# An attention and gated-MLP block on one core: outputs transposed in place, head sets in pairs, and queue orders from a table

## The chip, the cores and the metric

The kernel runs on one core of a Trainium2 chip. The core has a tensor engine (PE, with its weight loads PEld), a vector engine (DVE), a scalar engine (ACT), GpSimd (POOL) and a sync engine (SP), each with an instruction queue of its own that is worked off in order. The metric is device time in microseconds, the median of several runs. The profile shows one execution; its span runs from the first to the last instruction.

## The reference, cut to what matters

One layer over 2048 tokens of width 640, with 32 heads of width 20 and a hidden width of 1536:

```
mod = silu(c) @ w_mod;  sa, ca, ga, sb, cb, gb = its six parts
h = layernorm(x) * (1 + ca) + sa
q, k, v = split(h @ wqkv)                   # 32 heads x 20
p = softmax(q @ k.T * 20 ** -0.5)           # per head, 2048 x 2048
x = x + ga * (concat(p @ v) @ wo)
h = layernorm(x) * (1 + cb) + sb
x = x + gb * (((h @ w_gate) * (h @ w_up)) @ w_down)
```

Of the work, 32 x 2048 x 2048 exponentials are the largest single part.

## The kernel before, in words

**Chunks, items, units.** Queries are cut into seven chunks (CHUNKS): one of 512 and six of 256. Heads go in eight sets of four; the four heads of a set lie in the four 32-row strips of a tile. A chunk and a set make an item (`items`), worked in order. Within an item a unit is one head's scores of 512 columns: one tile of 128 keys by 512 queries in chunk 0, two tiles of keys by 256 queries in the others. The last item is split into two halves of 128 queries (SPLITJ, with QHALF).

**Two ways to an exponential.** Scores are products of KT and QT (line 1524) into PSUM banks. Most units go to ACT: two units, 1024 columns, per instruction (line 1561, called E), written to the ring PPs. Two pairs of banks take turns, so that a score group waits for the exponential before last. QUADS says how many quads of four units in each item go to DVE instead: an eviction with a rounding into integers (line 1585, called P1) for each unit, two bit operations over the quad (1617 and 1625) and a product (1622 on DVE or, in four pieces, 1637 on POOL). A quad's result comes as two terms, and each is multiplied with V.

**Products with V.** Line 2192 multiplies the exponentials with Vf, four strips side by side, and sums them in one bank for each item (a slot of G, four banks, which also serve the quads' scores and all projections). Vf holds a column of ones in front of each head, so the sums of the softmax come with the outputs.

**The end of an item** (`item_end_tasks`). DVE transposes the bank in blocks of 32 by 32 into OT (line 1717, T1), takes reciprocals (1723), POOL or DVE multiplies (1725, into OTn), and DVE transposes back into OcT (1734). Its rows, 32 a head, have to be packed to 20 a head: `oc_pieces` cuts the item into runs of rows and one DMA on SP for each run copies it into Ocp (line 1746). A chunk has 32 heads of which four cross a border of 128 rows, so 36 copies; for the last chunk's last set there is no copy, and four products with wo7, a second, padded copy of the last rows of wo, use OcT directly. wo is loaded by one DMA (line 1492) and wo7 by four.

**The suffix of a chunk** (`suffix`): the product with wo (line 970 or 966), the second layernorm, transposes (1889), then for each of twelve columns of 128 the gate and up products, with weights brought by DMA into three staging buffers (stg, line 1931). For chunks of 256, gate and up of one column share a bank; DVE evicts the gate half to gsb (1959) and multiplies it with the up half into hprod (1966). For chunk 0 each has its own bank (1986, 1997). Then the down product and the output. It runs beside the next chunk's attention; the last chunk's runs alone, the tail of the program.

**K and Q** are projected during chunk 0 (line 1230), packed, evicted to KPA or KPB, written to DRAM (line 1276) and loaded back spread over the strips (KT by line 1289, QT by 1298), because rows of 20 have to be spread to 32. All these DMAs are issued by SP, in its order.

**Who sets the order.** A planner in the kernel, `Sched`, simulates all engines when the program is built, with a duration for each task and guesses for DMA landings; `pick_pe` chooses what PE does next, and numbers by item (STAGE) tune the choices. The outcome is a fixed order of instructions on each queue, which `emit_program` writes out with the semaphore waits between them. Where little work would be on PE for a while, `do_fill` and `zero_fill` put in products with zeros (line 2523), called fillers.

Of the kernel before, what the change touches and what calls it, by code (L numbers as in the profile page):

```python
# [13 lines left out]
SEM = 60.0  # L14
# [4 lines left out]
X_FIRST = 0.0  # L19
ACT_LAT = 250.0  # L20
# [16 lines left out]
LKTOL = 300.0  # L37


class Task:  # L40
    __slots__ = ("head", "hval", "hknow", "eng", "dur", "lat", "deps", "emits", "ctr", "prio", "gate", "acq", "on_start", "slots",
                 "start", "done", "needed", "val", "know", "nleft", "ready", "users", "name", "mode", "seq", "rt", "sem",
                 "nbytes", "cond", "alt", "land", "firm", "lk", "dead", "key")

    def __init__(self, eng, dur, emits, deps=(), ctr=None, prio=0.0, lat=None, gate=0, acq=(), on_start=None,
# [28 lines left out]
        self.dead = False  # L74
        if lat is None:
            lat = {"pe": PE_DRAIN, "act": ACT_LAT, "dve": DVE_LAT, "pool": 60.0}.get(eng, 0.0)
        self.lat = lat

# [5 lines left out]
class Slots:  # L84

    def __init__(self, ids, name=""):
        self.name = name
        self.free = [(i, []) for i in ids]
        self.hold = {}
        self.gone = set()  # L90
        self.out = {}

    def avail(self, only=None):
        best = None
        for k, (i, rel) in enumerate(self.free):
            if only is not None and i != only:
                continue
            t = 0.0
            for r in rel:
                t = max(t, r.done + SEM)  # L100
            if best is None or t < best[0]:
                best = (t, k)
        return best
# [13 lines left out]
    def done(self, i, task):  # L117
        h = self.hold[i]
# [9 lines left out]
    def add(self, i, rel):  # L128
        self.free.append((i, rel))


class Sched:

    def __init__(self):
# [28 lines left out]
        self.lk_last = None  # L163

# [39 lines left out]
    def _enable(self, task):  # L204
        t = 0.0
        for d in task.deps:
            t = max(t, d.done + SEM)
# [70 lines left out]
    def step_engine(self, eng):  # L278
        if self.free_at[eng] > self.t:
            return False  # L280
        self.pull(eng)
        rl = self.readyl[eng]
        for k, task in enumerate(rl):
# [5 lines left out]
            if self.locked(eng, task):  # L289
                continue  # L290
            if self.acquire(task, self.t):
# [63 lines left out]

def emit_program(nc, sched, nsem_dma=56):
# [23 lines left out]
    for t in sched.all:  # L380
# [11 lines left out]
        for d in deps:  # L392
            if not (d.nbytes or d.eng != eng or d.eng in ("dve", "pool")):
                continue
            if d.head and eng == "act":
# [88 lines left out]
TB_GATE = 2  # L484
# [3 lines left out]
D_LEAD = 0.451  # L488
NB0, NSS = 3, 3
XB0, XSS = 0, 0  # L490
HEADG = 1000
OP_EARLY = 1
EV_OP = 0.5
# [3 lines left out]
LN2T = 0.6  # L497
# [5 lines left out]
HOLD = 110  # L503
PVTOL = 249
XDPRIO = 1.343
# [5 lines left out]
STX_G, STX_T, STX_S, W_ISSUE = 3, 20, 1.5, 600.0  # L511
ZFILL = 1
WD_POOL, WD_PRIO = 1, 400.0
# [4 lines left out]
WM_GATE = 8  # L518
# [3 lines left out]
K_LEAD = 0.683  # L522
# [3 lines left out]
D_LATE = 16  # L526
D_RES = 20
PVMIN, PVMAX, PVCAP = 2, 7, 12
PV0 = 0
V_PARTS = [[0, 2], [2, 4], [4, 6], [6, 8]]  # L530
V_L1 = 0.2
# [10 lines left out]
GATE_F = (0.446, 0.5, 0.5, 0.5, 0.5, 0.5, 1.0)  # L542
FILL_MIN = 4190.746
# [9 lines left out]
LN2P = 0.85  # L553
NALT = 1
OPFIRST = 1500
STG_B = 0.95
ENDP, END3, P_POW = 0.4, 1, -1.0
HT_L = 0.25
V_L = 0.221
LATE_A = 2.065  # L560
LATE_L = 1.418
LATEQ = (2, 3)
LATEQ_A = -20
LATEQ_F = 0.35
# [4 lines left out]
    0: {"PVMIN": 2, "HOLD": 95, "PVTOL": 249, "D_RES": 58, "PVCAP": 6, "X_HALF": 0.0, "XDPRIO": 1.343, "FILL_MIN": 3463.3, "LKTOL": 300.0, "EAGER": 9, "PVMAX": 14, "X_LATE": -179.96, "TPRIO": 0.75, "STEAL_GAP": 200, "D_LATE": 16, "PV_KEEP": 2},  # L569
    1: {"PVCAP": 15, "XBACK": 1, "FILL_MIN": 4629.7},  # L570
    2: {"DL": 0.376},
    4: {"HOLD": 58.0, "X_LATE": -39.3},
    5: {"D_LATE": 7, "PVMAX": 3},
    6: {"X_LATE": 168.4, "FILL_MIN": 5225.9, "HOLD": 156.4},
    7: {"DL": 0.501},
    8: {"FILL_MIN": 2868.8},
    10: {"X_HALF": 69.3, "HOLD": 73.7, "PVMAX": 5},
    11: {"DL": 0.443},
    12: {"DL": 0.459, "HOLD": 108.3, "X_LATE": 6.6},
    13: {"DL": 0.417},  # L580
    15: {"X_LATE": 86.8},
    16: {"HOLD": 135.0, "FILL_MIN": 4362.5},
    17: {"X_LATE": -17.4, "LKTOL": 338.9, "HOLD": 52.0},
    19: {"DL": 0.471, "PVMAX": 7, "HOLD": 113.6},
    20: {"DL": 0.391, "PVMAX": 10},
    21: {"X_LATE": -85.4, "PVMIN": 3},
    24: {"DL": 0.464, "STEAL_GAP": 210.6, "X_LATE": -52.5, "PVCAP": 14, "HOLD": 116.4, "LKTOL": 98.1},
    25: {"DL": 0.549, "LKTOL": 370.4, "HOLD": 156.3},
    26: {"DL": 0.411, "PVMIN": 1, "X_LATE": 2.0, "EAGER": 6, "X_HALF": 58.0},
    27: {"DL": 0.473},  # L590
    29: {"HOLD": 148.6, "D_LATE": 5, "LKTOL": 267.5, "D_RES": 36, "PVMAX": 3},
    30: {"EAGER": 11},
    31: {"X_LATE": -99.6, "HOLD": 173.2, "X_HALF": 164.9, "PV_KEEP": 2},
    33: {"DL": 0.442, "PVMIN": 7, "PV_KEEP": 3, "X_HALF": 147.4},
    34: {"PVMIN": 3, "X_HALF": 26.9, "STEAL_GAP": 91.8, "EAGER": 8, "X_LATE": 136.8, "D_RES": 25},
    35: {"X_HALF": 148.7},
    36: {"DL": 0.524},
    37: {"FILL_MIN": 4112.0, "EAGER": 8, "X_LATE": -201.5},
    39: {"STEAL_GAP": 162.9, "EAGER": 9},
    42: {"PVMAX": 8, "FILL_MIN": 4334.4, "PV_KEEP": 3},  # L600
    43: {"HOLD": 127.6},
    46: {"D_LATE": 20, "PV_KEEP": 3, "X_LATE": -80.9},
    53: {"LKTOL": 820.1, "X_HALF": 73.5},
    54: {"PVTOL": 279.6, "FILL_MIN": 4011.5, "X_HALF": 31.3},
}
XHALF = 1
STG_G0, STG_G, XC_G = 12, -10, -20
X_LATE = -24.052
X_HALF = 0.0
# [10 lines left out]
def build_kernel(nc, A_x, A_wqkv, A_wo, B_x, B_w_gate, B_w_up, B_w_down, c, w_mod, out):  # L620
# [96 lines left out]

    PPs = [alloc("PP", [128, NPS, w * 512], BF16) for w in ((3, 2) if HEADG < 1000 else (2, 2))]
    wo7 = alloc("wo7", [128, D], BF16)
# [9 lines left out]
    OTn = alloc("OTn", [128, 512], BF16)  # L729
    NOC = 2  # L730
    OcT = alloc("OcT", [128, NOC, 512], BF16)
    oc_off = region(2 * KD * 512 * 2)
    Ocp = at("Ocp", [128, 2, KD, 512], BF16, oc_off)
# [6 lines left out]
    late_off = region(late_size)  # L740
    early_off = region(early_size)
    R1 = Sub(late_off, late_size)
# [4 lines left out]
    R1 = Sub(early_off, early_size)  # L747
# [5 lines left out]
    R2 = Sub(early_off, early_size)  # L753
    hprod = R2.alloc("hprod", [128, FT, 512], BF16)
    h2T = R2.alloc("h2T", [128, KD, 512], BF16)
    xck = R2.alloc("xck", [128, 4, D], BF16)
    xn2 = R2.alloc("xn2", [128, 4, D], BF16)
# [8 lines left out]
    KPB = alloc("KPB", [128, 2, 512], BF16)  # L766
# [30 lines left out]
    G = Slots([5, 6, 2, 7], "G")  # L797
    GX = Slots([3, 4] if HEADG else [2, 3, 4], "GX")
    hx = (1, 3) if HEADG else (1, 3, 4)
    GC = Slots([0, 1], "GC")  # L800
    setA = Slots([0], "A")
    setB = Slots([0], "B")
    pPs = [Slots(list(range(NPS)), "PP") for _ in range(2)]

    def ring():
        return len(pPs[0].free) + len(pPs[1].free)
# [3 lines left out]
    sOcT = Slots(list(range(NOC)), "OcT")  # L810
# [407 lines left out]
    def k_base(tc):  # L1218
        return 80 if tc in K_DIRECT else 0
# [87 lines left out]
    def v_round(t, pt, prio, gate=0):  # L1307
        a, z = V_PARTS[pt]
        nh = 4 * (z - a)
        w = nh * DH  # L1310
        mms = []
        for k in range(KD):
            f = quarters(w, lambda k=k: hT[t // 4][:, k, t % 4 * 128:t % 4 * 128 + 128],
                         lambda k=k: wV[:, k, 80 * a:80 * a + w], k == 0, k == KD - 1)
            mms.append((X(w), f))

        def after(r):
            dst = Vf[:, (t * H + 4 * a) * VW:(t * H + 4 * a + nh) * VW].rearrange("p (h w) -> p h w", w=VW)[:, :, 1:VW]
            f = lambda e: e.tensor_copy(dst, ps[:, r.b["b"], 0:w].rearrange("p (h w) -> p h w", w=DH))
# [1309 lines left out]
```

## Time and profile before

| what | value |
|---|---|
| median of 3 runs | 806.06 us (804.76 to 808.96) |
| span of the profiled execution | 803.8 us |
| exponentials on ACT (line 1561) | 810, first start 16.4 us, last start 774.7 us |
| quads' evictions on DVE (line 1585) | 428, in 285.5 us |
| quads' products on POOL (line 1637) | 268 pieces, in 305.0 us |
| copies of line 1746 of the commonest size | 164, of 10.0 KB each |
| bytes moved by DMA | 64.66 MB, mean 80 GB/s |

Times are microseconds from the span's start. PE is the matrix products, PEld its weight loads; "SPq" is the queue of SP, on which it issues DMAs. An instruction's group is named by its line, what it writes and what it reads. A busy PE is not a PE at its peak, since products overlap.

### The profile page before, as it was taken

The page shows a single profiled execution, that of the slowest core. Times are in us where ns is not written, and L with a number is a line of the kernel's source. Part 1 is how long each engine was busy: PE and PEld are TensorE (multiplying, and loading weights), DVE is VectorE, ACT ScalarE, POOL GpSimd, SP SyncE. Part 2 cuts the span into 40 slices and gives each one's busy share as a digit, 9 for nine tenths or more (in the row PEclk, how much of TensorE's full clock was granted, in tenths as well). Part 3 has the DMA queues.
Part 4 walks back from the last instruction along what each step waited for, and adds up shares of the span by engine and source line. Part 5 has one row for each costly group of instructions (what it writes and reads, how often), then busy time and mean ns, then how long its engine had stood idle before and what let it go on. Part 6 is the DMA issues. An engine that isn't in the chain of part 4 may idle for free.

```text
span 803.8 us, 37761 instructions
## 1 busy us (share of the span) xinstructions
PE 790.4 (98%) x16595; PEld 380.6 (47%) x16595; DVE 697.8 (87%) x1401; ACT 764.8 (95%) x847; POOL 386.0 (48%) x396
## 2 busy tenths in 40 slices
PE   8999999999999999999999999999999999999998
PEld 4433433333244434445555455555555555555567
DVE  7978788799989999988999999999899988898754
ACT  6899899999999999999999999999999999999961
POOL 3347455654366565763444443545534554455300
PEclk9999999999999999999999999999999999999999
DMA  9733212212341532120032404231540254414420
GB/s 297 243 113 91 62 43 64 61 33 76 92 109 50 167 88 52 35 55 13 24 81 65 95 16 112 57 73 39 121 89 15 54 118 94 98 37 106 92 68 18
DMA packets 154314, 64.66 MB, mean 80 GB/s; under 512 B 116951, under 2 KB 154151, under 8 KB 154151
## 3 DMA queue, kind: packets, MB, share of 16 engines
q1 hardware_dynamic: 153223, 61.10, 30.0%
q8 instruction: 132, 2.16, 1.1%
q10 hardware_dynamic: 928, 1.15, 0.5%
q14 instruction: 31, 0.25, 0.1%
HBM read 50.63 MB, written 8.99 MB: 74 GB/s over the span
## 4 chain that ended last, share of the span: by engine, by line
PE 77%; ACT 14%; DVE 5%; issue 2%; DMA 1%; SPq 1%; POOL 0%; DVEq 0%; ACTq 0%
PE ps_all L1524 26%; PE ps_all L970 21%; PE ps_all L2192 19%; ACT PP L1561 14%; PE ps_all L1230 4%; PE ps_all L966 3%; DVE DB L1585 2%; PE ps_all L1889 1%; PE ps_all L1166 1%; PE ps_all L1127 1%; DVE DSS L1617 1%; PE ps_all L2523 0%; DVE DSS L1625 0%; DMA QT<-q_rows 0%; PE ps_all L991 0%
## 5 line engine op out<-in xcount | busy, mean ns | idle before, releaser
L1561 ACT ACTIVATE PP<-ps_all 128x1024 bf16<-128x1024 f32 x810 | 748.5, 1090 | 6.7 <-PE ps_all L1524 4.8
L1637 POOL TENSOR_TENSOR DSS<-DB,DSS 128x512 bf16<-128x512 bf16 x268 | 305.0, 1157 | 290.6 <-DVE DSS L1625 254.2
L1585 DVE TENSOR_SCALAR DB<-ps_all 128x512 int16<-128x512 f32 x428 | 285.5, 681 | 50.5 <-PE ps_all L1524 48.0
L1524 PE MATMUL ps_all<-QT,KT 32*128 32x256 bf16 (+2 forms) x3648 | 319.4, 287 | 4.5 <-DMA QT<-q_rows 0.8
L1524 PEld LDWEIGHTS ps_all<-QT,KT 32*128 32x128 bf16 x3648 | 93.9, 92 | 204.1 <-ACT PP L1561 141.5
L2192 PE MATMUL ps_all<-PP,Vf 128*32 128x256 bf16 (+2 forms) x2892 | 163.6, 291 | 0.5 <-DVE KPB L1242 0.3
L970 PE MATMUL ps_all<-h2T,stg 128*32 128x256 bf16 (+2 forms) x2716 | 122.9, 281 | 0.3 <-DVE DB L1585 0.2
L2192 PEld LDWEIGHTS ps_all<-PP,Vf 128*32 128x32 bf16 (+1 forms) x2892 | 54.5, 94 | 76.4 <-issue 67.6
L2192 PE MATMUL ps_all<-DSS,Vf 128*32 128x256 bf16 (+1 forms) x1512 | 88.7, 291 | 0.0
L1617 DVE TENSOR_SCALAR DSS<-DB 128x2048 int16<-128x2048 int16 x107 | 77.2, 722 | 0.8
L970 PEld LDWEIGHTS ps_all<-h2T,stg 128*32 128x32 bf16 x2716 | 61.6, 96 | 26.9 <-issue 22.0
L1625 DVE TENSOR_SCALAR DSS<-DB 128x2048 int16<-128x2048 int16 x107 | 73.2, 684 | 0.8 <-PE ps_all L2192 0.8
L970 PE MATMUL ps_all<-wd,hprod 128*32 128x320 bf16 (+1 forms) x1404 | 61.0, 277 | 0.0
L1725 POOL TENSOR_TENSOR OTn<-OT,invT 128x256 bf16<-128x256 f32 (+1 forms) x49 | 35.3, 721 | 37.7 <-DVE invT L1723 37.5
L1622 DVE TENSOR_TENSOR DSS<-DB,DSS 128x2048 bf16<-128x2048 bf16 x40 | 51.5, 1287 | 0.0
L2192 PEld LDWEIGHTS ps_all<-DSS,Vf 128*32 128x32 bf16 x1512 | 36.5, 95 | 20.9 <-issue 12.4
L970 PE MATMUL ps_all<-wV,hT 128*32 128x160 bf16 x1280 | 38.9, 236 | 0.9 <-DVE DB L1585 0.3
L970 PEld LDWEIGHTS ps_all<-wd,hprod 128*32 128x32 bf16 x1404 | 31.2, 96 | 14.2 <-issue 10.8
L1717 DVE STREAM_TRANSPOSE OT<-ps_all 128x256 f32<-128x256 f32 (+2 forms) x57 | 27.1, 475 | 8.8 <-PE ps_all L2192 8.5
L1230 PE MATMUL ps_all<-hT,wk 128*32 128x512 bf16 x360 | 32.3, 382 | 0.0
L970 PEld LDWEIGHTS ps_all<-wV,hT 128*32 128x32 bf16 x1280 | 24.6, 97 | 15.9 <-issue 8.2
L1230 PE MATMUL ps_all<-hT,wq 128*32 128x512 bf16 x375 | 31.3, 382 | 0.6 <-DVE OT L1717 0.6
(133 smaller groups left out, 556.1 us busy)
## 6 DMA issues: line engine op xcount, KB each, us to landing
stg<-in_B_w_gate_dram SPq DMA_DIRECT2D x74, 160.0 KB
stg<-in_B_w_up_dram SPq DMA_DIRECT2D x74, 160.0 KB
KT<-k_rows SPq DMA_DIRECT2D x112, 32.0 KB
QT<-q_rows SPq DMA_DIRECT2D x48, 64.0 KB
Ocp<-OcT SPq DMA_DIRECT2D x164, 10.0 KB
wm<-in_w_mod_dram SPq DMA_DIRECT2D x3, 800.0 KB
x<-in_A_x_dram SPq DMA_DIRECT2D x7, 320.0 KB
k_rows<-KPA SPq DMA_DIRECT2D x16, 128.0 KB
```

Of the source, the lines that this page charges most:

```text
L970: return lambda e, b: e.matmul(ps[32 * x:32 * x + 32, b, c0 + o:c0 + o + w], lhs()[:, 32 * x:32 * x + 32], rhs() if w == n else rhs()[:, o ...
L1230: f = [lambda e, b_, k=k, x=x: e.matmul(ps[x:x + min(32, w - x), b_, :], wx[:, k, r0 + x:r0 + min(x + 32, w)], hT[tc][:, k, :], tile_posit ...
L1524: ems.append(lambda e, i=i, kt=kt: e.matmul(dstf()[:, i * u.n:(i + 1) * u.n], KT[32 * u.s:32 * u.s + 32, u.j, kt * 128:(kt + 1) * 128], QT ...
L1561: return e.activation(PPs[g % 2][:, cellp["p"], 0:nu * 512], ps[:, b0:b0 + nu, :].rearrange("p b c -> p (b c)"), AFT.Exp, scale=ESCALE)
L1585: return e.tensor_scalar(DBl[st_["slot"]][:, x * 512:(x + 1) * 512], bank(cell["b"]), EBIAS, 0.0, op0=ALU.add, op1=ALU.max)
L1617: return e.tensor_scalar(DSl[st_["ss"][0]][:, :], DBl[st_["slot"]][:, :], 0x7F, 0x3F00, op0=ALU.bitwise_and, op1=ALU.bitwise_or)
L1622: return e.tensor_tensor(d, DBl[st_["slot"]][:, :].bitcast(BF16), d, ALU.mult)
L1625: return e.tensor_scalar(DSl[st_["ss"][1]][:, :], DBl[st_["slot"]][:, :], 0x7F80, 2, op0=ALU.bitwise_and, op1=ALU.bitwise_or)
L1637: return e.tensor_tensor(d, DBl[st_["slot"]][:, x * w:x * w + w].bitcast(BF16), d, ALU.mult)
L1717: t1 = Task("dve", n * 1.1 + 70, lambda e: e.transpose(OT[:, 0:n], ps[:, item_info[it]["bank"], 0:n].rearrange("p (b q r) -> p b r q", q=3 ...
L1725: f3 = lambda e: e.tensor_tensor(OTn[:, 0:n].rearrange("p (b c r) -> p b r c", c=32, r=2), OT[:, 0:n].rearrange("p (b r c) -> p b r c", c= ...
L2192: ems.append(lambda e, i=i, kt=kt, stt=stt, stp=stp: e.matmul(ps[32 * s:32 * s + mc, bk, 0:u.n], Vf[:, (kt * H + 4 * u.j + s) * VW:(kt * H ...
```

## The change

It does six things.

1. The second transpose writes straight into Ocp. OTn becomes a buffer for a whole chunk, packed 20 columns to a head, `[query block, 8 x 20, 2]`; the multiplication writes only the 20 columns that count (one instruction for each member of a pair), and as soon as a block of 32 packed columns is full, one transpose (f4) puts it into Ocp. The packed order is by strips, so the rows of wo are loaded in the same order, in 48 pieces in place of 1 and 4. OcT, wo7 and all copies of line 1746 are gone.
2. Head-set pairs (PAIRS): in chunks of 256, two neighbouring items (0 and 1, 2 and 3, ...) share one bank, 256 columns each. T1 and the reciprocal come once for a pair. The second's products start when those of the first have begun in all strips.
3. Gate and up of two columns of weights share a bank each (GU2): 512 columns per eviction and per product in chunks 1 to 5. Two more staging buffers for weights (MORE).
4. The exponentials' ring is 16 single buffers of 512 columns in place of eight of 1024 (`Ring`); `visit` forms score groups when PE comes to them, and may take the next units out of order (LOOK).
5. All of the planner's numbers are set anew: durations (LAT_X, REL_X, V_X, S_X), QUADS, and STAGE for each of the 57 items.
6. When the planner is done, `replan` drops 14 of PE's tasks, all fillers, and moves tasks within the five queues by a table (PLAN): 1302 moves on PE, 1 on ACT, 160 on DVE, 19 on POOL and 314 on SP.

```diff
-QUADS = ((0, 4, 3, 3, 3, 4, 4, 4), (2, 2, 1, 2, 2, 2, 1, 2), (2, 2, 1, 2, 2, 2, 1, 2), (2, 2, 1, 2, 2, 2, 1, 2), (2, 2, 1, 2, 2, 2, 1, 2), (2, 2, 1, 2, 2, 2, 1, 2), (2, 1, 2, 2, 2, 1, 2, 0))
+QUADS = ((0, 5, 3, 3, 3, 4, 3, 4), (2, 2, 2, 2, 2, 2, 1, 2), (1, 2, 1, 2, 2, 2, 1, 2), (1, 3, 1, 1, 2, 2, 1, 3), (2, 2, 1, 2, 3, 1, 1, 2), (2, 2, 1, 2, 2, 1, 2, 3), (2, 1, 2, 1, 1, 2, 4, 3))
...
+PLAN = {
+    "drop": (1824, 1840, 2170, 2543, 3239, 3248, 3259, 3812, 3825, 4391, 4823, 5109, 5110, 5487),
+    "pe": [
+        (129, 128), (153, 148), (154, 149), (156, 150), (208, 204), (191, 210), (192, 211), (193, 212), (226, 226), (229, 227),
...
+    "sp": [
+        (1, 0), (12, 10), (79, 16), (25, 19), (83, 20), (29, 21), (14, 22), (16, 23), (24, 25), (57, 27), (56, 28), (55, 29),
...
+def replan(sc):
+    gone = set(PLAN.get("drop", ()))
+    sc.order["pe"] = [t for i, t in enumerate(sc.order["pe"]) if i not in gone]
+    for eng, moves in PLAN.items():
+        if eng == "drop":
+            continue
+        old = sc.order[eng]
+        gone = {a for a, _ in moves}
+        new = [t for i, t in enumerate(old) if i not in gone]
+        for a, b in moves:
+            new.insert(b, old[a])
+        sc.order[eng] = new
...
+    lead, second = {}, {}
+    for it in range(len(items) - 1):
+        if PAIRS and items[it][1] % 2 == 0 and spans[it] == spans[it + 1] and spans[it][1] == 256:
+            lead[it + 1] = it
+            second[it] = it + 1
...
-    d_wo = [dma("sp", 128 * KD * D * 2, lambda e: e.dma_start(wo_sb[:, :, :], wov[:, :, :]), [d_wm[3][0]], prio=10)]
...
+                d_wo[i0 // 32].append(dma("sp", (i1 - i0) * D * 2, fwo, [d_wm[3][0]], prio=10 + .01 * i0))
...
-        t4 = dve(n * .55 + 65, lambda e: e.transpose(OcT[:, cell["s"], 0:n].bitcast(F32), OTn[:, 0:n].bitcast(F32)), [t3],
-                 prio=pe_)
...
-        for (b5, s, r0, nr, ro) in pcs:
-            def f(e, b5=b5, s=s, r0=r0, nr=nr, ro=ro):
-                return e.dma_start(Ocp[r0:r0 + nr, slot, b5, qo:qo + n],
-                                   OcT[32 * s + 1 + ro:32 * s + 1 + ro + nr, cell["s"], 0:n])
...
+            def f4(e):
+                o = Ocp[slot][:, b0:b1, qo:qo + nq_].bitcast(F32).rearrange("p k (b c) -> p k b c", c=32)
+                i = OTn[:, g0:g0 + gn, 32 * b0:32 * b1, :].rearrange("p b (k c) r -> p k b (c r)", c=32).bitcast(F32)
+                if nbk == 1:
+                    o, i = o[:, 0], i[:, 0]
+                return e.transpose(o, i)
+            t4 = dve(nq_ * nbk * .55 + 65, f4, dps, prio=pe_)
...
+                            f = lambda e: e.tensor_copy(gsb[:, gs, 0:2 * n], ps[:, r.b["b"], 0:2 * n])
...
+                            f = lambda e: e.tensor_tensor(
+                                hprod[:, fc - 1:fc + 1, 0:n], ps[:, r.b["b"], 0:2 * n].rearrange("p (a b) -> p a b", a=2),
+                                gsb[:, gs, 0:2 * n].rearrange("p (a b) -> p a b", a=2), ALU.mult)
...
     end = sc.run()
     sc.nhalf = nhalf[0]
+    replan(sc)
     nw = emit_program(nc, sc)
```

More of the change, by code (lines that the diff above doesn't have):

```diff
@@ L577 @@
[L577 to L587, printed above, removed]
@@ L2137, in pv_candidates @@
                     break
+            elif it in lead and any(first_pv[(lead[it], s)] for s in range(4)):
+                break
             na = 0
@@ L2250, in pv_issue @@
         for it in sorted(last):
-            if item_info[it]["left"] == 0:
-                t1 = t1s[it]
-                t1.deps = [last[it]]
+            o = own(it)
+            if all(item_info[x]["left"] == 0 for x in (o, second.get(o, o))) and not t1s[o].firm:
+                t1 = t1s[o]
+                t1.firm = True
+                t1.deps = [max(last.values(), key=lambda x: x.done)]
                 sc.left -= 1
```

918 lines of the change are left out of this document (615 added, 303 removed), and 197 rows, old and new, of the table PLAN.

## The prediction

> **What bounds the kernel now.** I read the page's busy shares first, then the line of the exponentials, then that line in stretches, then the chain of waits stretch by stretch.
>
> ```profile
> span 803.8 us, 37761 instructions
> PE 790.4 (98%) x16595; PEld 380.6 (47%) x16595; DVE 697.8 (87%) x1401; ACT 764.8 (95%) x847; POOL 386.0 (48%) x396
> ```
> Three engines are close to full, so the shares decide nothing. The exponentials split the span into three parts:
>
> ```profile
> L1561 ACT ACTIVATE PP<-ps_all x810: 1002/1067/1327, 16.4 to 774.7; 128x1024 bf16<-128x1024 f32 x162
>   PE ps_all L1524: 4.8, 12
>   PEld ps_all L1524: 141.5, 479
> ```
> (The first row gives the durations, the first and the last start; the second, what ACT sat idle for; the third, who waited for an exponential: us, times.) There are 810, the first at 16.4 us, the last from 774.7 to about 775.8. Before lies a head of 16.4 us, behind a tail of 28.0 us. ACT sits idle for scores only 4.8 us in all, and 479 times PE's score weights wait for an exponential to free its bank. In stretches of 100 us (length, ACT busy with them, their number, PE's granted clock, share and GB/s of DMA):
>
> ```profile
> 16.40:116.40 100.00, 90.65 (x98) 0.98 0.41 116
> 116.40:216.40 100.00, 99.94 (x109) 1.00 0.23 64
> 216.40:316.40 100.00, 99.33 (x108) 1.00 0.36 97
> 316.40:416.40 100.00, 99.64 (x109) 1.00 0.16 38
> 416.40:516.40 100.00, 99.78 (x109) 1.00 0.33 76
> 516.40:616.40 100.00, 99.94 (x109) 1.00 0.29 66
> 616.40:716.40 100.00, 99.69 (x110) 1.00 0.32 76
> ```
> From 116 to 716 us 654 exponentials take 600 us: 0.917 us each, in every stretch nearly alike. Only the first stretch is short, by 11. How fast could they go? In the last stretch the chain stays on ACT:
>
> ```profile
> 762.87 0.90 ACT PP L1561
> ...
> 771.01 1.20 ACT PP L1561
> ```
> The chain holds ten exponentials from the one row to the other (start, us), all on ACT but for pieces of up to 0.17 us; nine steps in 8.14 us, 0.904 us each. So 0.904 is ACT's own pace, and the steady 0.917 stands 1.4% above it: an exponential is often a little late, though ACT hardly shows idle time. Who makes it late, the chain of two stretches says (516 to 616 us, then the last):
>
> ```profile
> by line: PE ps_all L1524 35.7%; PE ps_all L970 35.5%; PE ps_all L2192 26.1%; DVE DB L1585 1.4%; PE ps_all L1889 1.1%; issue 0.5%
> by line: ACT PP L1561 43.2%; PE ps_all L1524 17.9%; PE ps_all L970 17.0%; PE ps_all L2192 12.5%; issue 6.5%; PE ps_all L966 3.0%; DVE xckc L1827 0.8%; ACTq L443 0.0%
> ```
> In the middle the chain is PE's order of scores, projections and products with V; at the end it is ACT. So PE and ACT are balanced within about 1%, DVE is hardly on the chain, and a gain needs both fewer exponentials and an order in which their scores come in time.
>
> **The change, part by part.** All sums are made on this execution's 803.8 us. The median of the three timed runs, 806.06, is 2.3 us above its span (804.76 to 808.96 in all); I subtract from the median.
>
> *Fewer exponentials.* Each quad moves four units of 512 columns from ACT to DVE. QUADS in before sums to 25 + 5x14 + 12 = 107 (the last entry of a 0 is replaced by QHALF). After: 25, 15, 13, 14, 14, 15 and, in the last chunk without its last entry, 13: 109. Two quads more are 8 units, 4 exponentials less: 806. From 16.4 to 775.8 one takes 759.4/810 = 0.938 us with all that comes between, so **-3.75 us** if all else keeps pace (4 x 0.904 = -3.6 at the floor). PE computes the same scores in four groups fewer, and 16 products with V more (8 units twice with two products each, less 8 once): four side by side at the 273 ns of a product of that shape (fillers, below), 1.1 us, against four changes between scores and products saved. I take 0.
>
> *Outputs straight into Ocp.* The 248 copies Ocp<-OcT (36 per chunk; 32 in the last, whose set 7 has none) leave SP; wo comes in 48 pieces instead of 5. What the copies cost shows at one place, where SP's order stands on the chain:
>
> ```profile
> 84.57 1.71 SPq L1276 DMA_DIRECT2D q_rows<-KPA  x3
> 86.33 1.24 SPq L1289 DMA_DIRECT2D KT<-k_rows  x1
> 87.61 2.98 SPq L1746 DMA_DIRECT2D Ocp<-OcT  x4
> 90.71 0.92 SPq L1298 DMA_DIRECT2D QT<-q_rows  x2
> ```
> The chain runs through them, on to the load's transfer (second row: how long a write of Q rows took elsewhere):
>
> ```profile
> 90.71 3.51 DMA QT<-q_rows
> ...
> 229.60 2.30 DMA q_rows<-KPB
> ```
> And the exponentials in the 20 us around it:
>
> ```profile
> 86.40:106.40 20.00, 16.62 (x18) 0.91 0.18 47
> ...
> 96.40:106.40 10.00, 8.50 (x10) 0.83 0.01 2
> ```
> Four copies hold the QT load for 2.98 us; it lands at 94.2 and PE's scores start there. ACT loses 3.38 of 20 us, and the clock falls to a mean of 0.83. Without the copies the load still waits for its own rows: their writes are issued by 86.28 (84.57 + 1.71), and at 2.30 us to land it could start at 88.6, 2.1 us earlier. Bounds: 0 (something else is put in the gap) to -3.4; I take **-2.1**. SP's issue time falls by about 205 x 0.745 us = 153 us over the span; that is cover, not time, except at this place. The 43 extra wo pieces are 32 us of SP in the first 200 us, where K and Q loads also pass; their price is the slower rival below.
>
> *DVE.* The groups with each shape apart (busy us, mean ns of one, idle before and its releaser):
>
> ```profile
> L1717 DVE STREAM_TRANSPOSE OT<-ps_all 128x256 f32<-128x256 f32 x47 | 20.8, 442 | 4.8 <-PE ps_all L2192 4.7
> L1717 DVE STREAM_TRANSPOSE OT<-ps_all 128x512 f32<-128x512 f32 x8 | 5.7, 712 | 1.4 <-PE ps_all L2192 1.3
> L1734 DVE STREAM_TRANSPOSE OcT<-OTn 128x128 f32<-128x128 f32 x47 | 14.2, 301 | 1.5 <-POOL OTn L1725 1.5
> L1734 DVE STREAM_TRANSPOSE OcT<-OTn 128x256 f32<-128x256 f32 x8 | 3.5, 433 | 0.0
> L1723 DVE RECIPROCAL invT<-OT 128x8 f32<-128x8 f32 x47 | 8.9, 189 | 0.2
> L1723 DVE RECIPROCAL invT<-OT 128x16 f32<-128x16 f32 x8 | 1.9, 241 | 0.1
> L1959 DVE CAST gsb<-ps_all 128x256 bf16<-128x256 f32 x60 | 24.6, 412 | 4.7 <-PE ps_all L970 4.6
> L1986 DVE CAST gsb<-ps_all 128x512 bf16<-128x512 f32 x12 | 8.1, 674 | 0.5 <-PE ps_all L970 0.5
> L1585 DVE TENSOR_SCALAR DB<-ps_all 128x512 int16<-128x512 f32 x428 | 285.5, 681 | 50.5 <-PE ps_all L1524 48.0
> L1617 DVE TENSOR_SCALAR DSS<-DB 128x2048 int16<-128x2048 int16 x107 | 77.2, 722 | 0.8
> L1725 POOL TENSOR_TENSOR OTn<-OT,invT 128x256 bf16<-128x256 f32 x42 | 27.9, 665 | 37.2 <-DVE invT L1723 37.0
> ```
> A pair of head sets needs one transpose of 512 (712 ns) for two of 256 (884) and one reciprocal (241) for two (378); the second transpose goes only over whole blocks of 32 columns, five per chunk, not eight items. A chunk of 256 saves 4x172 + 4x137 + (8x301 - 3x301 - 433) = 2.3 us, about 13 over all chunks with the last. Gate and up in pairs save 150 ns twice, 30 times: 9 us. Two quads add 8 x 667 ns (285.5 us over 428) and four bit operations of about 0.72: 8 us. Net about -14 of 698 us. This costs and earns nothing directly: DVE holds about 1% of the two chains above. It makes banks come free a little sooner. The second transpose still waits for POOL, now for both members; behind it on DVE stand the quads' evictions, whose banks PE wants. Before, that wait is 1.5 us in all 47. POOL's normalising in two strided pieces has no row; between the old 665 ns and twice that, beside a POOL that is busy 48%, it hides. A pair also keeps one bank until both members are done and delays the first member's output by an item; the output is needed only by the next chunk's work, and the pair holds one bank where two items held two.
>
> *Fillers.* Their line, and its busy time from 400 to 700 us:
>
> ```profile
> L2523 PE MATMUL ps_all<-ident,Vf x168: 272/273/391, 46.2 to 712.4; 128*32 128x256 bf16 x128, 128*32 128x512 bf16 x40
> ...
> 400.00:700.00 300.00, 0.00 (x0) 0.00 (x0) 1.00 0.33 75
> ```
> A filler is eight products of 256 columns or four of 512, so before has 128/8 + 40/4 = 26; at 273 ns and four side by side, a filler is at most two rounds, 0.55 us. From 400 to 700 us it has none. They stand where PE has time to spare. Fourteen out of the new plan's own number: 0 to -7.6 us (14 x 0.55), and by the clock a loss as well (rival). Being off PE's chain, I take **0**.
>
> That a quiet PE loses its clock is in the rows: 0.83 over ten microseconds is 1.7 us of clock gone, behind the late QT load. [...]
>
> *The orders.* Some 1,800 moves on five queues, hung on a finished plan. Here nothing in the trace gives the cost, only its ends. If every exponential from 116 to 716 us came at ACT's own pace, 654 x 0.013 = 8.8 us would go; if the order is no better, 0; and a move that lets an engine wait in line for a late load costs what the QT load cost, 3.4. The nearest row is the best stretch of before itself: 110 in 100 us, 0.909. All of them at that pace give 654 x 0.008 = **-5.3**, and I take that. What the first stretch loses besides the gap (100 - 90.65 - 3.38 = 6.0 us, in which ACT does other work or waits) I leave as it is: 0 to -6.
>
> *Tail.*
>
> ```profile
> L966 PE MATMUL ps_all<-wo,OcT 128*128 128x320 bf16 x4 | 1.0, 302 | 0.1
> ```
> These four products with wo7 go: 0 to -1.0 us. Two of them stand behind the last transpose, and two with Ocp's last block now stand in their place, so I take **0**.
>
> Sum: -3.75 - 2.1 - 5.3 = -11.15; 806.06 - 11.15 = **794.9 us**.
>
> **The rivals.**
> (B) *Only the exponentials go.* PE's order is the bound in the middle (97% of the chain from 516 to 616 us), a lighter DVE is hidden, and the QT gap is filled by wo pieces: 806.06 - 3.75 = 802.3. For it: the same pace in six stretches. Against it: 1.4% lateness with three engines that each have less to do.
> (C) *ACT's own pace.* All of 8.8, the whole 3.4 of the gap, 3.6 and 4 of the first stretch's other 6.0: -19.8, 786.3. For it: the 141.5 us in which PE waits for ACT, so PE has room. Against: PE busy at 98%.
> (D) *Slower: late loads.* Orders are fixed against planned landings; 43 more pieces on SP stand in front of K and Q rows, and PE waits in line. One late load costs 3.4 us as at 86 to 106. With the 11.15 won otherwise, the fourth such load turns the sign; six give 794.9 + 20.4 = 815. For it: SP is on the chain at that place today. Against: 248 copies leave the same queue.
> (E) *Slower: the clock.* Each filler that alone kept the clock costs 1.7 us. The seventh turns the sign; fourteen give 794.9 + 23.8 = 819. Against: the clock reads 1.00 in all stretches behind the first, also from 400 to 700 us, where not one filler stands.
>
> **How the numbers follow.** Forecast 0.55, B 0.14, C 0.18, D 0.09, E 0.04. A measurement of this kernel can tell about 0.5%, 4.0 us, from no change: 802.0 to 810.1. Faster: the forecast, C and half of B, 0.80. Same: the other half of B and the lighter cases of D, 0.10. Slower: the rest of D, and E, 0.10. The range reaches from C's 786 with one microsecond to spare, 785, to B with one late load, 802.3 + 3.4 = 805.7: 785 to 806, leaving out D, E and a little of C.
>
> **What would show it.** The exponentials' line: 806 of them, last start near 763 with a first start still near 16.4; 110 per stretch of 100 us (B: 109; C: 110 to 111). No Ocp<-OcT on SP, and no QT load as a row of the chain near 90 us; ACT with 10 to 11 in each 10 us there. DVE below 690 us. Clock rows at 1.00 behind 20 us (E: rows under 0.9; D: PE or ACT waiting for KT or QT by microseconds). It is wrong if the pace in the middle stays at 0.917, if the first stretch still holds 98, or if the tail grows past 28 us.

## The result and the profile after

The changed kernel takes **810.98 us** (median of 20 runs, 806.79 to 818.23) against 805.72 us of the kernel before (20 runs, 802.90 to 810.01, same chip). The ratio is **1.0062, 95% interval 1.0043 to 1.0081**: slower by 0.6%, where 794.9 us had been forecast, in a range of 785 to 806. The profiled execution took 811.48 us.

The page's first rows of the changed kernel, then the line of its exponentials (durations, first and last start; then who waited for them: us, times):

```profile
span 809.7 us, 37284 instructions
PE 791.5 (98%) x16536; PEld 375.1 (46%) x16536; DVE 694.3 (86%) x1276; ACT 759.8 (94%) x847; POOL 412.5 (51%) x416
```

```profile
L2913 ACT ACTIVATE PP<-ps_all x806: 1002/1177/1346, 18.5 to 778.2; 128x1024 bf16<-128x1024 f32 x162
...
  PEld ps_all L1933: 188.8, 666
```

There are 806 exponentials, as forecast, and PE's score weights wait for them more than before (188.8 us, not 141.5): scores stand ready earlier. But the first starts 2.1 us later and the last 3.5 us later. Counting how many have begun by 100, 140, 520, 540 and 760 us shows where. Before, then after (stretch, ACT busy with them, their number, clock, DMA):

```profile
0.00:100.00 100.00, 74.99 (x81) 0.98 0.55 162
0.00:140.00 140.00, 114.30 (x124) 0.99 0.45 131
0.00:520.00 520.00, 492.99 (x533) 1.00 0.32 85
0.00:540.00 540.00, 512.99 (x555) 1.00 0.32 84
0.00:760.00 760.00, 732.61 (x793) 1.00 0.32 82
```

```profile
0.00:100.00 100.00, 68.39 (x73) 0.98 0.52 153
0.00:140.00 140.00, 106.82 (x115) 0.98 0.41 121
0.00:520.00 520.00, 486.01 (x528) 0.99 0.30 80
0.00:540.00 540.00, 503.59 (x547) 0.99 0.30 80
0.00:760.00 760.00, 723.47 (x787) 1.00 0.31 78
```

Differences of these rows tell the story. Up to 140 us the changed kernel falls 9 exponentials behind, some 8.3 us at 0.92 each. From 140 to 520 it does 413 where before did 409; from 540 to 760 it does 240 where before did 238: the gain in the middle came. From 520 to 540 it does 19 against 22. At 760 us it has 19 left, before had 17; the 19 take 19.3 us, the 17 took 15.8, so 1.6 us more go there at the pace of before. Behind the last one the tail is 30.4 us (809.7 - 779.3) instead of 28.0. Together: 8.3 - 5.5 (six exponentials more in the middle) + 2.8 + 1.6 - 3.7 (four exponentials fewer) + 2.4 = 5.9 us, the difference of the two spans.

The largest loss lies between 80 and 110 us. Ten-microsecond stretches of the exponentials after:

```profile
80.00:90.00 10.00, 8.79 (x10) 1.00 0.36 95
90.00:100.00 10.00, 4.11 (x5) 0.81 0.23 61
100.00:110.00 10.00, 8.43 (x10) 0.85 0.07 18
```

SP's queue and PE's scores there, from the timeline of the changed kernel (start, length of the issue, number):

```profile
82.20 0.35 SPq L1653 DMA_DIRECT2D k_rows<-KPA  x1
85.25 0.31 SPq L1666 DMA_DIRECT2D KT<-k_rows  x1
...
86.52 4.87 SPq L1666 DMA_DIRECT2D KT<-k_rows  x6
91.43 0.39 SPq L1902 DMA_DIRECT2D wo<-in_A_wo_dram  x1
91.86 1.27 SPq L1653 DMA_DIRECT2D q_rows<-KPA  x2
...
93.88 0.35 SPq L1666 DMA_DIRECT2D KT<-k_rows  x1
```

```profile
97.19 0.61 PE L1933 MATMUL ps_all<-QT,KT 32*128 32x512 bf16 x3 [3.49 <-DMA KT<-k_rows]
```

A head's K needs four loads from rows whose write landed at 85.2. Three of them go out among the first rows behind it; the fourth stands behind loads for later heads, pieces of wo and the writes of Q rows, and goes out at 93.88, 8.6 us after it could. PE arrives at 93.7 and stands in line for 3.49 us. Then the clock is 0.81 and 0.85 over 20 us, 3.4 us of clock gone: microsecond by microsecond it reads 0.63 from 96 us, 0.50 in each of the six behind and 0.96 from 103 us, in all 6.8 us at half.

### The profile page after: what moved, and what is told of

Its sections match the earlier page's. It is cut to its first block, busy times and chain, and to the rows that moved or that the text cites. A ratio compares the mean times of both kernels' runs of the same rounds, so it can differ in the third digit from the quotient of the medians.

```text
span 809.7 us, 37284 instructions
## 1 busy us (share of the span) xinstructions
PE 791.5 (98%) x16536; PEld 375.1 (46%) x16536; DVE 694.3 (86%) x1276; ACT 759.8 (94%) x847; POOL 412.5 (51%) x416
## 4 chain that ended last, share of the span: by engine, by line
PE 55%; ACT 28%; DVE 7%; issue 5%; DMA 2%; SPq 1%; POOL 1%; ACTq 0%
ACT PP L2913 28%; PE ps_all L1933 19%; PE ps_all L1347 16%; PE ps_all L2613 12%; PE ps_all L1607 3%; PE ps_all L1343 3%; DVE DB L1960 3%; DVE DSS L1996 1%; POOL DSS L2016 1%; DMA k_rows<-KPA 1%; PE ps_all L3104 1%; SPq L1666 1%; DVE DSS L2004 1%; DMA KT<-k_rows 1%; PE ps_all L1504 1%
## 5 line engine op out<-in xcount | busy, mean ns | idle before, releaser
L2016 POOL TENSOR_TENSOR DSS<-DB,DSS 128x512 bf16<-128x512 bf16 x296 | 347.4, 1198 | 297.4 <-DVE DSS L2004 249.1
L1933 PEld LDWEIGHTS ps_all<-QT,KT 32*128 32x128 bf16 x3648 | 94.4, 92 | 220.2 <-ACT PP L2913 188.8
L2613 PE MATMUL ps_all<-PP,Vf 128*32 128x256 bf16 (+3 forms) x2876 | 164.6, 289 | 0.0
L2613 PE MATMUL ps_all<-DSS,Vf 128*32 128x256 bf16 (+3 forms) x1544 | 97.3, 290 | 0.4 <-POOL DSS L2016 0.2
L2613 PEld LDWEIGHTS ps_all<-PP,Vf 128*32 128x32 bf16 (+1 forms) x2876 | 67.4, 95 | 48.1 <-issue 41.3
L1996 DVE TENSOR_SCALAR DSS<-DB 128x2048 int16<-128x2048 int16 x109 | 82.7, 758 | 1.8 <-PE ps_all L2613 0.3
L2004 DVE TENSOR_SCALAR DSS<-DB 128x2048 int16<-128x2048 int16 x109 | 76.2, 699 | 0.9 <-PE ps_all L2613 0.9
L2613 PEld LDWEIGHTS ps_all<-DSS,Vf 128*32 128x32 bf16 (+1 forms) x1544 | 41.6, 96 | 17.8 <-issue 12.0
L2001 DVE TENSOR_TENSOR DSS<-DB,DSS 128x2048 bf16<-128x2048 bf16 x35 | 44.7, 1278 | 0.2
L2098 POOL TENSOR_TENSOR OTn<-OT,invT 128x160 bf16<-128x160 f32 (+1 forms) x44 | 23.0, 542 | 18.5 <-DVE invT L2093 18.3
L1607 PE MATMUL ps_all<-hT,wk 128*32 128x512 bf16 (+1 forms) x360 | 31.3, 384 | 0.0
L1347 PE MATMUL ps_all<-wo,Ocp 128*32 128x320 bf16 (+1 forms) x660 | 28.5, 282 | 0.2 <-DVE Ocp L2130 0.2
```

Of the source, the lines that this page charges most:

```text
L1347: return lambda e, b: e.matmul(ps[32 * x:32 * x + 32, b, c0 + o:c0 + o + w], lhs()[:, 32 * x:32 * x + 32], rhs() if w == n else rhs()[:, o ...
L1607: f = [lambda e, b_, k=k, x=x: e.matmul(ps[x:x + min(32, w - x), b_, :], wx[:, k, r0 + x:r0 + min(x + 32, w)], hT[tc][:, k, :], tile_posit ...
L1933: ems.append(lambda e, i=i, kt=kt: e.matmul(dstf()[:, i * u.n:(i + 1) * u.n], KT[32 * u.s:32 * u.s + 32, u.j, kt * 128:(kt + 1) * 128], QT ...
L1996: return e.tensor_scalar(DSl[st_["ss"][0]][:, :], DBl[st_["slot"]][:, :], 0x7F, 0x3F00, op0=ALU.bitwise_and, op1=ALU.bitwise_or)
L2001: return e.tensor_tensor(d, DBl[st_["slot"]][:, :].bitcast(BF16), d, ALU.mult)
L2004: return e.tensor_scalar(DSl[st_["ss"][1]][:, :], DBl[st_["slot"]][:, :], 0x7F80, 2, op0=ALU.bitwise_and, op1=ALU.bitwise_or)
```

## The experiments

Every time below is a median, with its ratio to runs of the kernel before that were made beside it, and the ratio's 95% interval. The medians of before lie between 804.50 and 805.83 us, so two kernels are compared by their ratios; 0.1% is 0.8 us. **Theory A**: the table's fixed order on SP makes loads late, and the rest of the change gains. **Theory B**: the rest of the change costs, the table helps.

### Which part: the table, SP's moves, its first stretch, the fillers

No table at all:
```
+    plan = {}
+    gone = set(plan.get("drop", ()))
...
+    for eng, moves in plan.items():
```


> The whole table of moves and dropped fillers is taken out; the outputs into Ocp, the pairs of head-sets, the two-part gate/up products and the retuned planner stay. Theory A (the table's order on SP makes loads late, the rest of the change gains): the 25 exponentials between 80 and 110 us go back to about 31 (+5 us earned), the first exponential starts near 16.5 instead of 18.5 (+2), and the middle pace falls back from 0.908 to about 0.917 us per exponential (600 of them: 5 lost): about 808 to 810 us, no QT or KT wait over 1.5 us. Theory B (the rest of the change is what costs, the table only helps): over 813 us, with the stall near 90 us still there. If the table brought nothing at all in the middle: about 804.


Measured: 808.47 us, 1.0039 (1.0011 to 1.0067). The counts of this kernel:

```profile
0.00:100.00 100.00, 69.87 (x76) 1.00 0.55 159
0.00:140.00 140.00, 109.87 (x120) 1.00 0.44 127
0.00:520.00 520.00, 488.71 (x532) 1.00 0.30 80
0.00:540.00 540.00, 505.87 (x551) 1.00 0.31 81
0.00:760.00 760.00, 725.80 (x791) 1.00 0.31 79
```

The time is where A put it, but for another reason. The middle stayed fast (412 from 140 to 520, 240 from 540 to 760), so **the better pace isn't the table's**; and the first stretch recovered only 3 of 8 exponentials, so the planner's own order is worse there too. The loss from 520 to 540 us (19) is there without the table as well: it belongs to the rest of the change. Theory B's 813 falls, but this part of B stays. Against the changed kernel (1.0062) the intervals overlap: what the table costs as a whole is not clear of the noise.

Only SP's moves out:
```
+    plan = {k: v for k, v in PLAN.items() if k != "sp"}
...
```


> Only SP's 300 moves are taken out of the table; the moves of PE, DVE, ACT and POOL and the dropped fillers stay. Theory A (SP's fixed order is the cause): first exponential near 16.5, 30 or more exponentials between 80 and 110 us, middle pace stays 0.908: 802 to 805 us. Rival (PE's and DVE's moves fit only the SP order they were searched with, so other loads come late in line): several waits of 1 to 4 us of PE for KT or QT elsewhere, 808 us or more. Theory B (not the table): no better than 810.


Measured: 810.53 us, 1.0057 (1.0037 to 1.0078). Theory A's 802 to 805 falls; by the time alone both the rival (808 or more) and theory B (no better than 810) would fit. The trace speaks for the rival (PE's moves were made for SP's): with SP's own order PE waits 3.4 us in line for another KT load, 60 to 80 us holds 16 new exponentials instead of 21, at a clock of 0.74, and 73 have begun by 100 us, no more than before the edit.

The table only for tasks that the planner starts behind 110 us:
```
+    own = {k: [t for t in lst if t.start < 110000.0] for k, lst in sc.order.items()}
...
+    for k in own:
+        sc.order[k] = own[k] + [t for t in sc.order[k] if t.start >= 110000.0]
```


> The planner's own order on all engines for everything that it starts before 110 us; the table's order and its dropped fillers from there on. Theory A (what the table loses it loses in the first 110 us): 76 exponentials begun by 100 us as without the table, 98 by 120, and a tail of 30.4 us behind the last exponential as with the table instead of 31.9: 806 to 807 us. Rival (the moves behind 110 us lose as well): 809 us or more.


Measured: 807.98 us, 1.0043 (1.0024 to 1.0062), 75 begun by 100 us, 97 by 120: between A's 806 to 807 and the rival's 809, and not to be told apart from no table at all.

The fillers back:
```
+    was = list(sc.order["pe"])
...
+    for j in sorted(PLAN["drop"]):
+        o = sc.order["pe"]
+        o.insert(o.index(was[j - 1]) + 1, was[j])
```


> The 14 dropped fillers are put back behind the tasks that they followed; all moves stay. Theory (they lie in ACT-bound stretches behind 254 us, at a granted clock of 1.00): the time stays within 0.5 us of the changed kernel's 811. Rival (without them the clock dips): 2 us or more faster. Second rival (PE has no room for them: 14 times 0.216 us): 3 us slower.


Measured: 811.56 us, 1.0080 (1.0057 to 1.0104). The rival by which their loss slowed the clock falls: with them it is no faster. The other's 3 us more are not seen (1.4 us by the ratios, 0.6 by the medians), but six runs don't shut them out. Nothing measurable hangs on the fillers.

### Which transfers: the stretch from 80 to 100 us

Four KT loads and the Q rows' writes first, 26 SP rows reordered:
```
+    o = sc.order["sp"]
+    first = [81, 84, 87, 95, 91, 92, 94]
+    sc.order["sp"] = o[:81] + [o[i] for i in first] + [o[i] for i in range(81, 107) if i not in first] + o[107:]
```


> One stretch of SP's order is changed, 26 transfers between 85 and 100 us: the four KT loads that the next K head needs are issued first, then the three q_rows writes, then the rest as before. Theory A (the KT load issued 8.6 us after its row write had landed is the stall): the wait of PE for KT at 93.7 to 97.2 us goes, the granted clock stays 1.00 there, 90 to 110 us holds 20 exponentials or more instead of 15, 4 to 5 us earned: 806 to 807 us. Rival (the transfers pushed back become late instead, or PE has no spare time to use it): under 1.5 us earned, 810 us.


Measured: 810.75 us, 1.0064 (1.0040 to 1.0089). The rival held, and the profile names the transfer. PE's waits from 20 to 115 us (us, times, longest), then a piece of the chain:

```profile
PE ps_all L2616 <- DVE Vf L1706: 3.5, 1, 3.5
```

```profile
90.31 3.24 DMA q_rows<-Ocp
93.57 0.45 DVE Ocp L2133
94.01 0.22 DVE Vf L1706
94.23 0.04 issue
94.28 0.32 PE ps_all L2616
```

The wait for KT is gone, and an equal one for Vf stands in its place. q_rows are filled with zeros read out of Ocp, and the outputs are now transposed straight into Ocp: DVE's first such block must not overwrite the zeros before that transfer has read them. This edit had sent the transfer 4.7 us later (90.31 instead of 85.60); DVE waited at the block, and V for PE stood behind it.

The same with the zero fill (row 82) kept early:
```
-    first = [81, 84, 87, 95, 91, 92, 94]
+    first = [81, 82, 84, 87, 95, 91, 92, 94]
```


> As the run with the K loads first, but the transfer that fills q_rows with zeros out of Ocp keeps its early place: in that run it went out 4.7 us later, the first block written into Ocp had to wait for it, and PE stood 3.5 us for Vf behind it on DVE. Theory A (single transfers that SP issues late make the stalls between 80 and 100 us, one behind the other): no wait of PE over 1.5 us between 60 and 110 us, the clock 1.00 there, 80 or more exponentials begun by 100 us counted with the late start (73 in the changed kernel), 4 to 5 us earned: 806 us. Rival (PE has too much work in that stretch, a third load is late next): 75 or fewer by 100 us, 810 us.


Measured: 806.92 us, 1.0034 (1.0012 to 1.0056), 78 begun by 100 us, clock 1.000 over the span. The one row of SP's queue is worth 2.4 us by the ratios and 3.8 us by the medians, with intervals that overlap; that the wait for Vf is gone shows in the trace. A QT load is the next to be late, by 0.9 us.

Only the 15 pieces of wo out of this stretch, put behind the QT loads:
```
+    o = sc.order["sp"]
+    wo = [t for t in o[60:107] if t.emits[0].__name__ == "fwo"]
+    sc.order["sp"] = o[:60] + [t for t in o[60:107] if t not in wo] + wo + o[107:]
```


> Of the changed kernel's SP order only the 15 pieces of wo that stand between 63 and 98 us are put behind the QT loads, ahead of SP's idle stretch; nothing else moves. Rival D as it was predicted (pieces of wo ahead of K rows are what makes the loads late): the 3.5 us wait for KT goes, 806 us. Theory A (some 5 us of SP's time go to other K loads and to q_rows writes; the pieces cost 0.3 to 0.4 us each): the KT load goes out 1 to 2 us earlier, the wait shrinks to about 2 us: 808.5 to 810 us.


Measured: 806.85 us, 1.0032 (1.0016 to 1.0047), 77 begun by 100 us, no wait for KT. This is the size that the prediction's rival D gave (806), not my smaller one (808.5 to 810): the KT load goes out 2.6 us earlier (91.28 instead of 93.88), 1.1 us of it the three pieces behind 86 us and 1.2 us because the six KT loads ahead of it took 3.64 us to issue instead of 4.87, and 2.6 us was enough.

### The head

c ahead of x again, and its exponential ahead of ACT's two scalings:
```
+    sc.order["sp"][:2] = sc.order["sp"][1::-1]
+    o = sc.order["act"]
+    o.insert(5, o.pop(7))
```


> Two moves at the very start: SP issues c ahead of x again, and ACT's exponential of c stands ahead of its two scalings of x instead of behind them. Theory A (late c lets the clock go cold and puts scol behind ACT's scalings): the column rounds start near 8 instead of 10.3 us, the first of the 806 exponentials near 16.4 instead of 18.5, and the whole is 1.5 to 2 us shorter: 809 us. Rival (the head is hidden, since PE is busy 791 of 810 us and a stall behind it takes the gain): the first exponential earlier, but under 0.7 us earned: 810.5 us.


Measured: 809.16 us, 1.0057 (1.0033 to 1.0081). PE's fillers and the column rounds behind them, in the changed kernel and then here:

```profile
5.17 5.30 PE L3104 MATMUL ps_all<-ident 128*128 128x512 bf16 x12
10.26 0.85 PE L1368 MATMUL ps_all<-scol,wm 128*128 128x1 bf16 x25
```

```profile
3.88 3.17 PE L3107 MATMUL ps_all<-ident 128*128 128x512 bf16 x12
8.69 0.78 PE L1371 MATMUL ps_all<-scol,wm 128*128 128x1 bf16 x25 [1.64 <-DVE scol L1393]
```

The same 12 fillers take 5.30 us behind the late c and 3.17 us behind the early one, and they stand in line ahead of the rounds. PE stood 1.22 us for the late c and not for the early one; that this gap left the fillers slow is argued from these two runs, since the clock reads 1.00 in every row of both heads. The first exponential comes at 16.9 instead of 18.5 us. But by 100 us only 74 have begun, one more than in the changed kernel: the late KT load takes the gain, as the rival said. The median is the theory's 809, but by the ratios only 0.4 us are earned.

Both mends together:
```
+    first = [81, 82, 84, 87, 95, 91, 92, 94]
...
+    sc.order["sp"][:2] = sc.order["sp"][1::-1]
...
+    o.insert(5, o.pop(7))
```


> Both mends together: c issued ahead of x and its exponential ahead of ACT's two scalings; four KT loads, the zero fill and the three q_rows writes ahead of the rest between 85 and 100 us. Theory A: the two gains add up, 2 exponentials from the head and 5 to 6 from the stretch, 80 or more begun by 100 us: 803.5 to 805 us. Rival (the gain of the head is eaten at the next stall, as it was when c alone was first): no better than the K loads alone.


Measured: **805.70 us, 1.0005 (0.9988 to 1.0021)**: level with the kernel before, 0.7 us above theory A's range and by the ratios 2.3 us below the K loads alone. Some 4.6 us of loss (1.0062 to 1.0005) hung on ten places in SP's queue and one on ACT.

### Why level, and not faster

With both mends, the QT load forward and POOL's last two pieces of a shared quad free of a wait:
```
+    first = [81, 82, 84, 87, 95, 91, 92, 94, 86, 88, 89, 103, 99]
...
+        if t.name == "XP.107":
+            t.deps = [d for d in t.deps if d.name in ("M.107", "EX.107")]
```


> As the run with both mends (c first, K loads and zero fill first), and two more: the QT load that PE waited 1.3 us for goes out five rows earlier, and the last two POOL pieces of the last shared quad no longer wait for DVE's OTn (POOL stood 1.85 us for it, then shared 3.6 us with a DVE X). Theory A: the QT wait goes (1 us), the last PV products come 1.5 us earlier and the span ends up to 1.5 us earlier: 803 to 804 us, level with the kernel before or 0.2% under it. Rival (behind the last exponential PE's own line of products is the bound): the tail stays 30 us, 805 us.


Measured: 804.96 us, 1.0010 (0.9997 to 1.0023). The QT wait is gone; the counts:

```profile
0.00:100.00 100.00, 73.71 (x79) 1.00 0.53 154
0.00:140.00 140.00, 113.71 (x123) 1.00 0.44 126
0.00:520.00 520.00, 492.86 (x536) 1.00 0.30 80
0.00:540.00 540.00, 510.45 (x555) 1.00 0.31 81
0.00:760.00 760.00, 730.34 (x795) 1.00 0.32 80
```

At 760 us 11 exponentials are left where before has 17. The last one ends at 772.2 us, 3.6 us ahead of before, and yet the span ends only 1.4 us ahead (802.4): the tail is 30.2 us. The rival held (the tail stays, 805 us), not the theory's 803 to 804. Three exponentials are still lost at 520 to 540 us. Two runs, both on top of these mends, asked after these two places.

```
+    o[3670:3693] = o[3680:3684] + o[3670:3676] + o[3684:3693] + o[3676:3680]   # PE, near 530 us
+    o[5553:5586] = o[5575:5586] + o[5553:5575]                                 # PE, the tail
```
(with POOL's last pieces near 530 us free, two DVE evictions exchanged and the last transposes forward)


> All four mends of the run with POOL freed, and three more at two places. Near 530 us, where ACT stands 2.4 us because all 16 probability slots wait for PV products: POOL's last two pieces of that shared quad no longer wait for DVE's normalised x, PE takes four of that quad's products and nine PV products up to 0.8 us earlier, and DVE evicts the block whose bank they need first. In the tail: the last head set's PV products and its transposes go ahead of the last down products. Theory (the stall is a queue of POOL, DVE and PE places, each a little late): 20 to 21 exponentials between 520 and 540 us instead of 19, the tail 0.5 us shorter: 803.5 to 804.5 us. Rival (DVE is full there, 19.8 of 20 us, and the bank comes no earlier): 19 again, 805 us.


Measured: 806.10 us, 1.0015 (0.9999 to 1.0031): 19 again from 520 to 540 us, no shorter tail. The rival's number came, but its reason, a full DVE, is not shown: DVE is busy 19.80 of these 20 us in the changed kernel, but 18.87 in this run with the same 19, and 19.06 in the kernel before with its 22. In the changed kernel ACT waits 2.40 us at 530 us for a PV product, since the probability slots are full; PE works off 40 gate and up products (1.34 us) ahead of it, and waits for banks that DVE evicts add some 0.4 us. With these moves ACT still waits 1.91 us there.

```
+    need = {id(d) for lst in sc.order.values() for t in lst for d in t.deps}
+    o = sc.order["pe"]
+    sc.order["pe"] = o[:5475] + [t for t in o[5475:] if t.name not in ("dn5.0", "dn5.1") or t.deps or id(t) in need]
```


> All four mends, and 42 of the 50 groups of the down products of the last but one chunk are left out (168 matmuls; the output of that chunk is then not the reference's). Theory (behind the last exponential PE's own line is the bound, so what the faster middle left undone is paid in full there): 4 us off the span, about 801 us, the tail at 26 us. Rival (the tail waits for DVE's and POOL's chain of statistics, the products only fill it): under 1.5 us, 803.5 us or more.


Measured: 806.19 us, 1.0012 (0.9991 to 1.0033). Nothing earned by leaving out 168 products (1.0010 with them): PE's own line isn't the bound behind the last exponential. What these products did is seen one step on. The same 94 products, nearly all of the gate and up projections, from the chain with the down products (the run before this) and without:

```profile
780.52 5.58 PE ps_all L1359 x94
```

```profile
779.54 7.22 PE ps_all L1355 x94
```

The run before this has other moves in its tail too. In the kernel with POOL free, from which only the down products are missing here, the chain gets to these products at 778.85 us, 0.7 us earlier than without them. And without them they run slower. The clock in that kernel, then here:

```profile
779.50:782.00 2.50, 2.45 (x42) 1.00 0.00 0
```

```profile
779.50:782.00 2.50, 2.46 (x23) 0.54 0.00 0
```

The down products filled a wait of PE for DVE's and POOL's statistics (1.56 us here), and with them the clock stayed at 1.00.

## Why the prediction was wrong, by its steps

- **Fewer exponentials, -3.75.** The count was right (806), and with the loads mended the last one ends 3.6 us earlier. The step failed in "if all else keeps pace": the quads that replace them are DVE's and POOL's, and the last chunk's output waits for their PV products. In the mended kernel (all mends, POOL free) DVE hands PE the transposed, normalised rows of the final chunk 6.6 us behind the last exponential (778.8 - 772.2), before 4.9 us behind it (780.7 - 775.8): 1.7 of the 2.2 us by which its tail is longer. Of the 3.6 us, 1.4 reached the end. Why, the traces suggest: DVE's transpose of the last chunk's set 6, which has four quads instead of two, came 13.4 us ahead of the end of the last exponential (775.8 - 762.4); in the mended kernel it comes 1.6 us ahead (772.2 - 770.6). That the last quads cause it is read from the traces; no run isolates it. The two transposes, before and then mended:

```profile
762.35 0.45 DVE L1717 STREAM_TRANSPOSE OT<-ps_all 128x256 f32<-128x256 f32 x1 [0.42 <-PE ps_all L2192]
```

```profile
770.61 0.45 DVE L2096 STREAM_TRANSPOSE OT<-ps_all 128x256 f32<-128x256 f32 x1 [0.84 <-PE ps_all L2622]
```

- **Outputs straight into Ocp, -2.1.** The copies went and with them the late QT load, but I priced the place, not the queue: a KT load is late in the same stretch, by more. The bound of 0 ("something else is put in the gap") was no bound: the term can be a loss. By 100 us 8 exponentials are missing; with the pieces of wo out of this stretch four of them are back, with the K loads forward five. The part also brought a new wait that I had not listed, the first block behind the zero fill out of Ocp.
- **DVE, -14 us, worth nothing.** Right for the change without its table: 682.5 us against 697.8. The table gave 11.8 back (694.3), half of it in one group, whose instructions became longer; from the groups of DVE without and with the table (busy, mean ns):

```profile
L1997 DVE TENSOR_SCALAR DSS<-DB 128x2048 int16<-128x2048 int16 x109 | 76.8, 704 | 0.7
```

```profile
L1996 DVE TENSOR_SCALAR DSS<-DB 128x2048 int16<-128x2048 int16 x109 | 82.7, 758 | 1.8 <-PE ps_all L2613 0.3
```

- **Fillers, 0.** Right; rival E fell, the clock is 1.00 in every stretch from 110 us to the last exponential. Its 1.7 us for each filler was an estimate from the one late QT load, and no run shows such a loss: with the 14 back the ratio is 1.0080, without them 1.0062.
- **The orders, -5.3.** This is the step that turned the sign. The pace came (653 exponentials against 647 from 140 to 520 and 540 to 760 us, 5.5 us). That the size fits the -5.3 is luck: my 654 counted an exponential that crosses the edge of two stretches in both. Taken as one stretch the 600 us hold 649, 0.924 us each and not 0.917, and the "best stretch" with 110 was no faster than those with 109 (ACT busy 99.69 us in it, in two of those 99.94). And the gain isn't the orders': it comes without the table too, and 2.8 us of it go again at 530 us. The table itself earned nothing that can be measured: 810.98 us (1.0062) with it, 808.47 (1.0039) without, the intervals overlapping. What it did was rival D's price, given a chance of 0.09: one transfer 8.6 us late, 3.5 us of standing in line and 3.4 us of clock. ACT lost 7.5 of the 20 us from 90 to 110, where a load had been priced at 3.4.
- **The first stretch's other 6.0 us "as is", and the tail, 0.** Both moved: the head came 2.1 us later, 1.6 of them for c behind x and its exponential behind ACT's scalings, and the tail is 2.4 us longer.

What stays open: which of the pairs, the two-part gate and up products and the retuned planner makes the middle faster, and which loses the three exponentials at 530 us. Switching one off replans everything behind it, so no run was made of it.

## What to carry to other kernels

A queue that issues in order prices each transfer by what stands behind it: moving eight rows of SP forward by a few microseconds was worth 2.3 us (1.0062 to 1.0034), and mending one late load showed the next of the same size, so mend them until the wait list is empty and only then judge a change. A gain read as a pace is kept only if the stages before and behind it don't give it back: count the paced instructions at a few times and measure head and tail apart. Moves hung on a finished plan must carry the waits that the plan put in for timing alone.

## What the runs showed of the hardware

With c behind x at the very start the fillers behind it took two thirds longer (12 in 5.30 us instead of 3.17), and with 168 products left out others ran at a lower clock (0.54 instead of 1.00 over 2.5 us; 94 took 7.22 us, not 5.58). DVE and POOL slowed each other. In the changed kernel's tail POOL's pieces of X stood for DVE and then ran beside DVE's own X; freed, they ran earlier, and X alone. POOL and DVE of the changed kernel, then of the kernel with POOL free:

```profile
773.85 3.62 POOL L2016 TENSOR_TENSOR DSS<-DB,DSS 128x512 bf16<-128x512 bf16 x2 [1.85 <-DVE OTn L2098]
774.28 2.18 DVE L2001 TENSOR_TENSOR DSS<-DB,DSS 128x2048 bf16<-128x2048 bf16 x1
```

```profile
762.59 4.95 POOL L2025 TENSOR_TENSOR DSS<-DB,DSS 128x512 bf16<-128x512 bf16 x4
768.16 1.21 DVE L2010 TENSOR_TENSOR DSS<-DB,DSS 128x2048 bf16<-128x2048 bf16 x1
```

X took 2.18 us beside POOL and 1.21 alone; a POOL piece took 1.81 beside X and 1.24 in the row without it. The plan holds POOL back while such a DVE operation runs; the table's moves took some of these operations elsewhere and left POOL waiting for the wrong one. No piece of POOL took over 1.168 us before and none over 1.167 in the change without the table; with the table the longest took 2.198.
